# Splitting one weight load in two and moving its second half behind two others, at the start of a fused transformer block

## Chip, cores, metric

One core of one Trainium2 chip. The metric is the device time of one execution in microseconds (us), of the slowest (here the only) core. The profile's span, from the first to the last instruction, is about 1.8 us shorter than that time. Engines: PE multiplies matrices, PEld is its weight load, DVE, ACT and POOL are the vector, scalar and GpSimd engines; SP issues nearly all DMA. A load runs on 16 DMA engines; each signals when its part is in, and the load has landed with the sixteenth signal.

## The reference, cut to what matters

```python
mod = (_silu(c) @ w_mod).reshape(c.shape[0], 6, 1, -1)     # w_mod: 1024 x 6144
sa, ca, ga, sb, cb, gb = (mod[:, i].copy() for i in range(6))   # shortened
h = _layernorm(x) * (1 + ca) + sa
x = x + ga * linear_attention(h, wqkv, wo)      # x: 2048 x 1024, 32 heads
h = _layernorm(x) * (1 + cb) + sb
x = x + gb * swiglu(h, w_gate, w_up, w_down)    # inner width 3584
```

Everything is bf16. The change concerns `sa`, the shift of the first normalisation: a 1024 x 1024 block of `w_mod`, columns 0 to 1023, called wsa here.

## The kernel before: the parts concerned

A small scheduler records each operation and works out semaphore waits; all operations therefore carry one source line in the profile (L176), and one goes by the names of tiles. SP issues loads in program order:

```python
def sa_load(p):       # p = 0: columns 0-511, p = 1: columns 512-1023; 1 MB in rows of 1 KB
    P.dma("wsa%d" % p, WSA[:, :, 512 * p:512 * p + 512], wmv[:, :, 512 * p:512 * p + 512])
def wq_load(i, n=1):  # 256 KB per i, in rows of 2 KB
    P.dma("wq%d" % i, WQK[:, i:i + n, 0:D], wqkvv[:, i:i + n, 0:D])

ca_load(0); wq_load(0, 2); wq_load(2, 2); ca_load(1); wq_load(4, 2)
sa_load(1); wq_load(6); wq_load(7); sa_load(0)
for j in range(2):
    P.dma("x1_%d" % j, XRES[:, 4 + j, :], xv[:, 4 + j, :])
# ... more loads
```

PE uses wsa three times between parts of the first q product (`q_part`, one matmul of 512 columns for each column block nt and row block dt). `mod_sc` multiplies 128-column blocks of wsa by silu(c), with one moving column each; `bias_mm` folds the shift of row blocks 0 to 5 into a bias of q:

```python
for nt in range(7):
    if nt == 4:
        mod_sc(WSA, 0, range(6, 8))      # first use: columns 768-1023
        fin_sa(6, 2)                     # DVE copies the result out
        for dt in (6, 7): h0_scale(dt)   # DVE makes row blocks 6 and 7
    q_part(nt, qb[nt], (4, 5))
mod_sc(WSA, 0, range(4, 6))              # second use: columns 512-767
fin_sa(4, 2, True)
for nt in range(7):
    if nt == 2: bias_mm((4, 5))
    q_part(nt, qb[nt], (6,))
for nt in range(7):
    if nt == 1:
        mod_sc(WSA, 0, range(4))         # third use: columns 0-511
        fin_sa(0, 4, True)
        ln_ops[1][0](); ln_ops[1][1]()   # DVE statistics of the x load x1_1
    if nt == 4:
        bias_mm(range(4)); bias_fin()    # bias_fin: DVE copies the bias out
    q_part(nt, qb[nt], (7,))
# ... then the last column block of q, which needs the bank that the bias leaves
```

## Time and profile before

| | before |
|---|---|
| median of 3 runs | 830.8 us (830.74 to 831.32) |
| span, PE busy | 829.4 us, 823.2 us |
| right half of wsa: issue, landing | 7.79, 20.88 us |
| left half of wsa: issue to landing | 13.79, 11.5 us |
| PE at first, second, third use | 20.93, 22.64, 25.30 us |

The lines themselves stand in the prediction. They are read so: a `DMA` piece in the chain of waits ends where PE could go on; a row of the order of time gives the start of a group, its length, and in brackets the idle time ahead of it.

### The profile page before, as it was taken

How to read it: one execution, taken by the hardware profiler on the slowest of the kernel's cores; microseconds unless marked ns; L12 is line 12 of the kernel's file. 1: busy time of each engine (PE TensorE's matmuls, PEld its weight loads, DVE VectorE, ACT ScalarE, POOL GpSimd, SP SyncE). 2: the span in 40 equal slices, each digit the busy share in tenths (PEclk: the TensorE clock that was granted, in tenths of full speed). 3: DMA queues.
4: the chain of work that ended last, by engine and by line, in shares of the span. 5: the costliest groups of instructions: out<-in, count | busy, mean ns of one | idle time of the engine just before them, and what ended most of it. 6: DMA issues, size and time to landing. Idle time of an engine off the chain costs nothing.

```text
span 829.4 us, 10017 instructions
## 1 busy us (share of the span) xinstructions
PE 823.2 (99%) x4083; PEld 378.8 (46%) x4083; DVE 312.6 (38%) x665; ACT 197.5 (24%) x336; POOL 39.9 (5%) x57
## 2 busy tenths in 40 slices
PE   8999999999999999999999999999999999999998
PEld 4544444444444444444444444444444444444444
DVE  5797986756955521121221112122111211221111
ACT  4757641323242111011111101111110111111011
POOL 1010000000130000030000003000000300000000
PEclk9999999999999999999999999999999999999999
DMA  9969656938397985700455571045557004553000
GB/s 321 287 151 231 148 159 171 201 104 304 60 256 229 276 264 158 192 25 15 124 155 150 153 185 33 16 124 153 154 151 190 26 18 123 154 152 87 0 26 26
DMA packets 199246, 119.28 MB, mean 144 GB/s; under 512 B 57881, under 2 KB 182945, under 8 KB 199201
## 3 DMA queue, kind: packets, MB, share of 16 engines
q1 hardware_dynamic: 199184, 118.65, 52.8%
q8 instruction: 32, 0.52, 0.3%
q14 instruction: 14, 0.11, 0.0%
q10 hardware_dynamic: 16, 0.00, 0.0%
HBM read 100.67 MB, written 4.33 MB: 127 GB/s over the span
## 4 chain that ended last, share of the span: by engine, by line
PE 97%; DMA 2%; SPq 1%; issue 0%; DVE 0%
PE ps L176 97%; DMA wsa<-in_w_mod_dram 2%; SPq L176 1%; DVE xres L176 0%
## 5 line engine op out<-in xcount | busy, mean ns | idle before, releaser
L176 PE MATMUL ps<-h2t,gug 128*128 128x512 bf16 x896 | 211.7, 379 | 0.0
L176 PE MATMUL ps<-h2t,guu 128*128 128x512 bf16 x896 | 211.7, 379 | 0.0
L176 DVE TENSOR_TENSOR at<-sg,ps 128x512 bf16<-128x512 bf16 x112 | 77.0, 687 | 282.8 <-PE ps L176 281.2
L176 ACT ACTIVATE sg<-ps 128x512 bf16<-128x512 f32 x112 | 66.9, 597 | 309.7 <-PE ps L176 309.7
L176 PEld LDWEIGHTS ps<-h2t,guu 128*128 128x128 bf16 x896 | 87.6, 98 | 105.7
L176 PEld LDWEIGHTS ps<-h2t,gug 128*128 128x128 bf16 x896 | 87.7, 98 | 105.5
L176 PE MATMUL ps<-wd_a,at 128*128 128x512 bf16 (+1 forms) x512 | 112.4, 377 | 0.0
L176 PE MATMUL ps<-ht,wqk 128*128 128x512 bf16 x512 | 111.7, 379 | 0.0
L176 PE MATMUL ps<-wd_b,at 128*128 128x512 bf16 (+1 forms) x384 | 85.0, 377 | 0.0
L176 PEld LDWEIGHTS ps<-wd_a,at 128*128 128x128 bf16 x512 | 50.1, 98 | 59.6
L176 DVE TENSOR_TENSOR ut<-att,gb_b 128x512 bf16<-128x512 bf16 (+1 forms) x32 | 14.3, 447 | 166.8 <-ACT att L176 166.8
L176 PEld LDWEIGHTS ps<-ht,wqk 128*128 128x128 bf16 x512 | 49.5, 98 | 58.7 <-DVE biasq L176 0.2
L176 ACT ACTIVATE att<-ps 128x512 bf16<-128x512 f32 (+1 forms) x32 | 17.4, 591 | 182.1 <-PE ps L176 182.1
L176 PEld LDWEIGHTS ps<-wd_b,at 128*128 128x128 bf16 x384 | 37.6, 98 | 44.7
L176 PE MATMUL ps<-pk,xres 128*128 128x512 bf16 x256 | 56.5, 379 | 0.0
L176 PE MATMUL ps<-mw,pqt 128*128 128x512 bf16 x256 | 56.3, 379 | 0.0
L176 POOL TENSOR_SCALAR h2t<-h2t,modcol 128x512 bf16<-128x512 bf16 x32 | 26.3, 836 | 383.4 <-DMA h2t<-xn 383.4
L176 ACT ACTIVATE e<-ps 128x512 bf16<-128x512 f32 x56 | 33.1, 603 | 31.7 <-PE ps L176 19.8
L176 PEld LDWEIGHTS ps<-mw,pqt 128*128 128x128 bf16 x256 | 24.9, 98 | 30.2 <-DVE xres L176 0.4
L176 PEld LDWEIGHTS ps<-pk,xres 128*128 128x128 bf16 x256 | 24.9, 98 | 29.9 <-issue 0.4
L176 ACT ACTIVATE junk<-xres 128x1024 bf16<-128x1024 bf16 x24 | 25.4, 1058 | 35.1 <-DVE xres L176 34.9
L176 DVE SCALAR_TENSOR_TENSOR xres<-ps,xres 128x512 bf16<-128x512 f32 x32 | 21.4, 688 | 12.3 <-PE ps L176 11.5
(107 smaller groups left out, 344.8 us busy)
## 6 DMA issues: line engine op xcount, KB each, us to landing
gug<-in_B_w_gate_dram SPq DMA_DIRECT2D x56, 512.0 KB, 4.0
guu<-in_B_w_up_dram SPq DMA_DIRECT2D x56, 512.0 KB, 5.3
xres<-in_A_x_dram SPq DMA_DIRECT2D x20, 256.0 KB, 7.7
rb<-recip_den SPq DMA_DIRECT2D x8, 512.0 KB, 11.5
stgx<-in_w_mod_dram SPq DMA_DIRECT2D x2, 2048.0 KB, 7.9
wd_a<-in_B_w_down_dram SPq DMA_DIRECT2D x4, 1024.0 KB, 7.8
out_dram<-xres SPq DMA_DIRECT2D x31, 128.0 KB, 1.7
xres<-in_A_x_dram SPq DMA_DIRECT2D x3, 1024.0 KB, 14.1
```

What stands on the lines that cost most here:

```text
L176: return getattr(e, method)(**kw)
```

## The change

PE's first use needs only a quarter of wsa, columns 768 to 1023. The intent: load that quarter alone, so that the first use and q weights 6 and 7 get their data 0.5 MB sooner, and bring columns 512 to 767 behind them.

```diff
-        def sa_load(p):
-            P.dma("wsa%d" % p, WSA[:, :, 512 * p:512 * p + 512], wmv[:, :, 512 * p:512 * p + 512])
+        def sa_load(c0, c1):
+            P.dma("wsa%d" % c0, WSA[:, :, c0:c1], wmv[:, :, c0:c1])
 ...
-        sa_load(1)
+        sa_load(768, 1024)
         wq_load(6)
         wq_load(7)
-        sa_load(0)
+        sa_load(512, 768)
+        sa_load(0, 512)
```

## The prediction

> **What bounds the kernel now.** I read the page first, then the chain of waits that ended last, then the waits of the TensorE, then the order of time on PE and PEld between 17 and 28 us, then the times from DMA issue to landing, and last the DMA rate in stretches that carry rows of one length.
>
> ```profile
> PE 823.2 (99%) x4083; PEld 378.8 (46%) x4083; DVE 312.6 (38%) x665; ACT 197.5 (24%) x336; POOL 39.9 (5%) x57
> ```
>
> PE is busy 823.2 of 829.4 us. So only the few us of this span in which PE stands still can be won, and only from a wait that really stops it. The chain in order of time says where the last such wait is:
>
> ```profile
> 7.79 13.09 DMA wsa<-in_w_mod_dram
> 20.88 0.05 issue
> 20.93 805.88 PE ps L176 x3932
> ```
>
> The right half of the shift weights (wsa, columns 512 to 1023) is issued at 7.79 and lands at 20.88, PE starts at 20.93, and from there the chain is PE to the end. Whatever moves PE after 20.93 moves the end by as much, unless a later wait takes it back. The list of waits names that same load, for 0.2 us (`PE ps` waiting for `DMA wsa`), and no other load that the change touches. But the recorded length of a matmul is longer than its turn, so short stalls hide in it, and the starts have to be compared:
>
> ```profile
> 17.09 3.61 PE L176 MATMUL ps<-ht,wqk 128*128 128x512 bf16 x16
> 20.93 0.55 PE L176 MATMUL ps<-siluc,wsa 128*128 128x1 bf16 x16 [0.23 <-DMA wsa<-in_w_mod_dram]
> 21.34 1.46 PE L176 MATMUL ps<-ht,wqk 128*128 128x512 bf16 x6
> 22.64 0.54 PE L176 MATMUL ps<-siluc,wsa 128*128 128x1 bf16 x16
> 23.04 0.59 PE L176 MATMUL ps<-ht,wqk 128*128 128x512 bf16 x2
> 23.56 0.55 PE L176 MATMUL ps<-modtmp,wqk 128*128 128x1 bf16 x16
> 23.98 1.46 PE L176 MATMUL ps<-ht,wqk 128*128 128x512 bf16 x6
> 25.30 0.95 PE L176 MATMUL ps<-siluc,wsa 128*128 128x1 bf16 x32
> ```
>
> A matmul of 512 columns lasts 0.379 us in the record but starts 0.216 us after the one before: (3.61 - 0.379)/15 = 0.215. Sixteen of them from 17.09 put the next start at 17.09 + 16 x 0.2155 = 20.54. PE starts at 20.93: the real stall is 0.39 us, not 0.23. After the six from 21.34 the next start would be 22.64, and it is 22.64: the second use of wsa (columns 512 to 767) waits for nothing. After the six from 23.98 the next start would be 25.28, and it is 25.30. This third use, columns 0 to 511, looks free, but the weight loads say otherwise:
>
> ```profile
> 22.42 0.66 PEld L176 LDWEIGHTS ps<-siluc,wsa 128*128 128x128 bf16 x16
> 25.29 0.87 PEld L176 LDWEIGHTS ps<-siluc,wsa 128*128 128x128 bf16 x32 [0.35 <-DMA wsa<-in_w_mod_dram]
> ```
>
> At 22.42 the load of weights begins 0.22 ahead of its matmul, beside the matmul before it; at 25.29 it begins with its matmul, having waited for the DMA. Issue 13.79 plus 11.5 to landing is 25.29. So the left half of wsa lands just in time, with no slack at all.
>
> **What the Trainium skill says.** "TensorE: Matmul & The Clock Gate", section "Step-by-step: what each phase is for", gives about 216 ns between back-to-back matmuls of 512 columns and says that weight loads are pulled ahead of running matmuls; the trace agrees (0.2155 us, and 22.42 against 22.64). "Perfetto Trace Analysis", section "Optimization Strategies", says that splitting DMAs lets some start sooner where the DMA engines are generally idle. They are not idle here (windows below), so its condition fails. "DMA: Bandwidth & Descriptors", section "Specifications", puts line rate at 512 B and over; section "Why small descriptors are slow (HBM only)" counts about 3 cycles per packet on top of one per 32 B. By that, two of 512 B cost 2 x (16 + 3) = 38 cycles against 35 for one of 1 KB, 9% more (estimate). The trace disagrees on both:
>
> ```profile
> 25.40:26.80 1.40, 1.40 (x38) 1.04 (x37) 0.33 (x3) 0.85 (x1) 0.00 (x0) 1.00 1.10 352
> 236.00:241.00 5.00, 5.00 (x25) 2.29 (x24) 2.84 (x11) 1.78 (x3) 1.61 (x2) 1.00 1.20 290
> ```
>
> The last two columns are DMA share and GB/s. In the first stretch nearly all packets are rows of 1 KB (352 GB/s); in the second all are rows of 512 B, loads of gate and up weights with the very shape 128x8x256 that the change introduces (290 GB/s). Both keep the engines full, so shorter rows cost 21%.
>
> **The change part by part.** It removes one load of 1 MB in rows of 1 KB (512 bf16 columns) and adds two of 0.5 MB in rows of 512 B. The order of the instructions on PE, DVE, ACT and POOL stays; the first use now waits for columns 768 to 1023, and the second has a new wait, for columns 512 to 767.
> - Cost of a half: 524,288 B at 290 GB/s is 1.81 us, at 352 it is 1.49. The difference is 0.32; the issues of gate and up loads, 1.78 us apart in that full queue, give 0.29. I take 0.30 each, 0.60 for both.
> - First use: the loads ahead of it lose 0.5 MB, so it lands near 20.88 - 1.49 + 0.30 = 19.7, before 20.54. The stall of 0.39 is gone; PE reaches the second use at 22.64 - 0.39 = 22.25.
> - Second use: its load now stands at the byte position where q weights 7 end. These land at 22.26 before (issue 12.96, 9.3 to landing). With 0.60 for the short rows: 22.86, and a start at 22.91. New stall 0.66. The second use thus starts 0.27 later than before.
> - Third use: the work between second and third use took 25.28 - 22.64 = 2.64, so PE is there at 25.55. All bytes ahead of this load are the same as before, so it lands at 25.29 + 0.60 = 25.89. PE starts near 25.90 instead of 25.30. Further stall 0.35.
> - Sum: - 0.39 + 0.66 + 0.35, less the 0.02 that the old third use waited, is + 0.60 us. Behind it all loads are 0.6 later, but PE too, so no new wait arises there; 435 matmuls from 27.56 run at 0.2158 us each without a hole, so nothing absorbs the shift either. The extra issue, about 0.43 us on SP, lies in a queue that is full for 11 to 13 us ahead and is hidden.
>
> So the change takes a wait away from the first use and pays for it at the third, whose landing no order of the loads ahead can move: only their bytes and row lengths can. 830.8 + 0.6 = 831.4 us.
>
> **The rivals.** (1) Short rows cost nothing in this mix, as the line-rate figure would have it: then the second use stalls about 0.06, the third lands where it did, the 0.39 is given back there, and the time is 830.8. For it: two short loads stand between loads of 2 KB rows, not in a long run of short ones. Against it: 290 GB/s is steady over 6 us. (2) The gain of 0.39 is kept, 830.4. For it: the chain names only the first load. Against it: the left half's landing at 25.29 with the weight load waiting for it. (3) The short loads cost more than their bytes, since the engines finish unevenly or the two DMAs' completions lie in the path: up to twice my 0.6, 832.0. (4) A late shift makes another engine the bound (ACT and DVE are busy from 28 us with the activation of q): both move with PE, so I give it little.
>
> **Range and chances.** The three timed runs before lie between 830.74 and 831.32, and the mechanism can give between - 0.4 and + 1.2. Predicted 831.4, range 830.6 to 832.1. Two per cent is 16.6 us and the whole disputed stretch is some 5 us long: faster 0.005, same 0.985, slower 0.01.
>
> **What would show it.** In the new trace: no stall ahead of the first use, PE there at about 20.54; a wait of PE for wsa of about 0.66 ahead of the second use (start near 22.9) and one of about 0.35 ahead of the third (start near 25.9); windows with rows of 512 B at about 290 GB/s in the stretch from 15.5 to 21. It is wrong if the third use starts at 25.3 or before (rivals 1, 2), or if the shift of the third use isn't found again at the end.

## The result, and the profile after

The changed kernel took 832.09 us in the median of 6 runs (831.61 to 832.63), the kernel before 830.88 in 6 runs of the same rounds (830.53 to 832.01). The ratio is 1.0012 with a 95% interval of 1.0000 to 1.0025. (Ratios are from runs of the same rounds; they are not quite the quotient of the medians, nor of the plain means.) It is "the same" by the 2% rule, and inside the predicted range, though only 0.01 us under its upper end. Two more sets of the changed kernel, below, gave 1.0007 and 1.0004. The mean of the three is 1.0008, or 0.6 us, against the predicted 0.6; each interval alone reaches down to 1.0000 or below, so the times alone do not prove a cost; the profiles below have to.

First the page's line of busy times, the chain of waits in order of time, and the TensorE in order of time (start, length, group, idle time ahead), all of the changed kernel:

```profile
PE 824.1 (99%) x4083; PEld 378.7 (46%) x4083; DVE 312.0 (38%) x665; ACT 197.6 (24%) x336; POOL 40.1 (5%) x57
```

```profile
15.71 10.69 DMA wsa<-in_w_mod_dram
26.40 0.05 issue
26.44 801.70 PE ps L176 x3870
```

```profile
17.90 3.61 PE L176 MATMUL ps<-ht,wqk 128*128 128x512 bf16 x16
21.35 0.54 PE L176 MATMUL ps<-siluc,wsa 128*128 128x1 bf16 x16
21.75 1.46 PE L176 MATMUL ps<-ht,wqk 128*128 128x512 bf16 x6
23.56 0.55 PE L176 MATMUL ps<-siluc,wsa 128*128 128x1 bf16 x16 [0.36 <-DMA wsa<-in_w_mod_dram]
23.98 0.59 PE L176 MATMUL ps<-ht,wqk 128*128 128x512 bf16 x2
24.50 0.55 PE L176 MATMUL ps<-modtmp,wqk 128*128 128x1 bf16 x16
24.91 1.46 PE L176 MATMUL ps<-ht,wqk 128*128 128x512 bf16 x6
26.44 0.95 PE L176 MATMUL ps<-siluc,wsa 128*128 128x1 bf16 x32
```

The last DMA of the chain is now the left half of wsa, which lands at 26.40; before, it was the right half. From the starts: the first use comes at 17.90 + 16 x 0.2155 = 21.35, so without a stall. The second would come at 21.75 + 6 x 0.2155 = 23.04 and comes at 23.56: 0.52 us of stall. The third would come at 26.20 and comes at 26.44: 0.24. So far this is the predicted picture.

Two things in it were not predicted. PE is 0.81 us later already at 17.90 (17.09 before), ahead of any load that was changed. And the third use is 1.14 us later (26.44 against 25.30), not 0.6. The signals of the 16 DMA engines, which the trace records for each load, show why. This table is not a view of the page; it is worked out from those records (us; first, fifteenth and sixteenth signal):

```
                             before                  changed
load                     1st   15th   16th       1st   15th   16th
scale weights, 2nd half  14.15  14.82  14.96     14.05  15.63  16.75
q weights 4, 5           15.52  16.18  16.33     15.43  17.04  18.12
wsa 512-1023             18.43  19.11  20.88         -      -      -
wsa 768-1023                 -      -      -     17.21  19.82  20.33
q weights 6              19.11  19.79  21.56     17.89  20.51  21.01
q weights 7              19.79  20.48  22.24     18.59  21.21  21.74
wsa 512-767                  -      -      -     20.30  23.00  23.52
wsa 0-511                22.80  23.47  25.25     23.31  25.92  26.40
```

Read the first column of each for what the bytes and rows cost: the left half of wsa comes 23.31 - 22.80 = 0.51 us later on the engine that is first. Read the distance to the sixteenth for how far the slowest engine has fallen behind: 2.45 us before, 3.09 changed. PE waits for the sixteenth. In the kernel before, fifteen engines had delivered the right half by 19.11, well ahead of 20.54, where PE wanted it. A single engine, 1.77 us behind the others, made the stall that the change was meant to remove.

That engine lost its time in a step, between q weights 4 and 5 (0.15 us between fifteenth and sixteenth) and the right half of wsa (1.77). In that stretch the DMA view of the kernel before has one packet of another queue (queue and kind: packets, MB, share of 16 engines):

```profile
q1 hardware_dynamic: 508, 0.52, 104.6%
q8 instruction: 1, 0.02, 4.6%
```

It is one packet of 16 KB, from 16.05 us, and takes 1.10 us. The page counts 32 of them in the span. The Trainium skill, "Runtime: NRT & Kernel Launch", section "Instruction fetch mechanics", says that each engine's instructions are refilled in blocks of 16 KiB (256 instructions) by a DMA queue of its sequencer, and that crossing a block is "mostly hidden". PE has 2 x 4083 = 8166 weight loads and matmuls, which would be 32 blocks (an estimate from the page's figure); that these packets are PE's instructions is inferred from this count, not shown. In the changed kernel such a packet came at 16.80 us and met another engine than the slowest: the fifteenth signal moves away from the first between q weights 4 and 5 and wsa 768-1023 (from 1.61 to 2.61 us). The slowest engine there was already behind, after the first x loads, where one packet of 2 KB took 1.00 us.

So a third term stands beside bytes and rows: the lag of the slowest of 16 engines, which differs from run to run.

### The profile page after: what moved, and what is told of

Same layout as the page of the kernel before. It is cut to its first block, busy times and chain, and to the rows that moved or that the text cites. A ratio compares the mean times of both kernels' runs of the same rounds, so it can differ in the third digit from the quotient of the medians.

```text
span 830.7 us, 10019 instructions
## 1 busy us (share of the span) xinstructions
PE 824.1 (99%) x4083; PEld 378.7 (46%) x4083; DVE 312.0 (38%) x665; ACT 197.6 (24%) x336; POOL 40.1 (5%) x57
## 4 chain that ended last, share of the span: by engine, by line
PE 97%; SPq 2%; DMA 1%; issue 0%; DVE 0%
PE ps L176 97%; SPq L176 2%; DMA wsa<-in_w_mod_dram 1%; DVE xres L176 0%
```

## The experiments

Theories, as the expectations call them. **A**: the end is set by the landing of the left half of wsa at the third use; short rows make it 0.5 to 0.6 us later, and the slowest engine's lag comes on top. **L**: short rows also make the slow engine fall further behind. **O**: not the rows but the new order, with its wait at the second use, is what costs. **N**: there is only noise, or something else sets the end. Theories **B** (half clock) and **F** (the instruction packet makes the lag) came up on the way. Times are medians, and each set was timed against the kernel before on the same chip.

**1 and 2. Both kernels again.** No edit.

> The kernel before, unchanged, as a second look. Theory A: the end is set by the landing of the left half of the shift weights at the third use on PE, and that landing is the time of the slowest of 16 DMA engines: one engine falls about 1.8 us behind the other 15 when the 16 KB packet on the instruction queue (near 16 us) takes its turn on it. Expected: ratio 1.000 (within 0.0006); in the trace again one engine that signals 1 to 3 us after the other fifteen for the load of the right half, on whichever engine the instruction packet hits; the first of the 16 signals of the third load near 22.8, the last between 24.5 and 26.5, and PE's third use within 0.1 us behind that last one. Rival N (noise alone): no such lone engine.

> The changed kernel again. Theory A: first signal of the third load near 23.3 (0.5 later than before, the price of 2048 short rows), the lag of the slowest engine 1.5 to 3.2 us as in any run, time +0.5 to +0.7 us over the kernel before (ratio 1.0006 to 1.0008). Rival L (short rows also make the slow engine fall further behind, by some 0.3 to 0.6 us more): +0.9 to +1.3 us (1.0011 to 1.0015). Rival N: ratio 1.000.

Before again: 831.1 us, ratio 1.0001 (0.9989 to 1.0013). Left half: first signal 22.89, last 25.11; third use 25.16. Here the lag is spread over several engines (the fifteenth signals at 24.11), so "one lone engine" was too simple, but the sixteenth again decides. Changed again: 831.38 us, ratio 1.0007 (0.9995 to 1.0019). First signal 23.53, last 25.27: later rows, but a lag of only 1.74 us, and the third use at 25.41 without any stall (24.12 + 6 x 0.2155 = 25.41). Its five runs fall into two heaps, 831.25 to 831.38 and 832.34 to 832.36. That fits A, but with an interval from 0.9995 it does not exclude N. It speaks against L: the lag was smaller than before's, not larger. Over all 14 profiles of this document the lag at the left half is 2.38 us in the mean of the 7 with short rows and 2.25 in that of the 7 without, which is much less than its scatter.

**3. Short rows alone, old order.**

```diff
         sa_load(768, 1024)
+        sa_load(512, 768)
         wq_load(6)
         wq_load(7)
-        sa_load(512, 768)
```

> Short rows alone: both halves of the right half in loads of their own, but both ahead of q weights 6 and 7 as before. Theory A: the third load lands as in the changed kernel, so the same time as the changed kernel, +0.5 to +0.7 us, though the stall now stands at the first use (near 0.9 us) and there is none at the second. Rival O (the new order, with its wait at the second use, is what costs): ratio 1.000. Rival L: as the changed kernel, +0.9 to +1.3.

832.02 us, ratio 1.0024 (1.0002 to 1.0046), with a first signal of the left half at 23.44 and the third use at 25.78, 0.5 us later than before. The cost of the rows is there without the new order, so O falls. There was no stall at the first use (20.89), against the expectation: this time the last signal of both quarters was in by 21.04, and PE needs only the first, in at 19.48. The mean is drawn up by two of six runs, of 833.71 and 838.31 us, with a mean clock of 0.998 and 0.996 where the others of the set have 1.0; the other four have a mean of 831.67, 0.54 above that of the kernel before (831.13). Even so, 838.31 is not explained by its clock alone, and no profile of it was kept.

**4. All four quarters short.**

```diff
-        sa_load(0, 512)
+        sa_load(256, 512)
+        sa_load(0, 256)
```

> The changed kernel with the left half (columns 0 to 511) split into two loads of 512 B rows too: 4096 short rows in place of 2048. Theory A: first signal of the last quarter near 23.8, time +1.1 to +1.3 us over before (twice the price of short rows, 1.0013 to 1.0016). Rival O or N: no more than the changed kernel. Rival L: +1.8 or more.

833.54 us, ratio 1.0022 (1.0009 to 1.0035), more than A allowed. First signal of the last quarter 24.26 (expected 23.8), 1.46 us later than before, so about 0.36 for each short load. The third use came at 26.06, only 0.76 us later than before's, because the lag happened to be 1.76. But from there to the end this profile took about 2 us more than the others. Engines' busy times by stretch (the last three columns are granted clock, DMA share, GB/s) say why:

```profile
25.00:28.60 3.60, 2.86 (x70) 2.06 (x70) 1.43 (x4) 1.87 (x3) 0.00 (x0) 1.00 1.09 357
28.70:32.00 3.30, 3.30 (x10) 1.22 (x8) 2.70 (x12) 3.30 (x8) 1.14 (x2) 0.50 1.07 365
```

After the stall at the third use PE's clock was granted at half, for 3.413 us. At half speed that costs 1.7 us. Three of the five runs had it (mean clock 0.998: 833.54 to 834.11), two did not (831.48, 832.70). This is theory B, made after the fact; runs 5 and 6 test it. (Another 0.38 us of this profile is a wait near 147 us, see run 9.)

**5 and 6. The third use later, without short rows.** The kernel before, with the left half behind one or two x loads of 256 KB.

```diff
-        sa_load(0)
         for j in range(2):
             P.dma("x1_%d" % j, XRES[:, 4 + j, :], xv[:, 4 + j, :])
+            if j == 0: sa_load(0)        # third_late_1
+        sa_load(0)                       # third_late_2: here instead
```

> The kernel before (rows of 1 KB), with the left half of the shift weights behind one x load of 256 KB (rows of 2 KB). Only the landing of the third use moves, by 0.68 us (the distance of the landings of q weights 6 and 7 in the trace of before). Theory A (that landing sets the end): PE's third use near 25.9 and +0.6 to +0.8 us, ratio 1.0007 to 1.0010. Theory B, on top of A (a stall of PE of about 0.9 us there drops its clock to half for 3.4 us, as in the profile of the kernel with all rows short): in some runs another 1.7 us with a mean clock of 0.998. Rival N (something else than the third use sets the end): 1.000.

> The same, behind two x loads of 256 KB: the landing moves by 1.36 us. Theory A alone: third use near 26.6, +1.3 to +1.5 us, ratio 1.0016 to 1.0018, clock 1.0. Theory B: the stall of about 1.3 us drops the clock in all or nearly all runs: +3.0 to +3.3 us, ratio 1.0036 to 1.0040, mean clock 0.998, with a stretch of 3.4 us at 0.5 from about 28 to 32 us. Rival N: 1.000.

One load: 832.05 us, ratio 1.0011 (0.9998 to 1.0024); three runs at full clock of 831.57 to 832.05, two at 0.998 of 833.18 and 833.55. Two loads: 834.28 us, ratio 1.0029 (1.0016 to 1.0043); four runs at 0.998 of 833.79 to 835.20, one at full clock of 832.45. The rows for two loads, TensorE in order of time and the stretch behind it:

```profile
24.25 1.45 PE L176 MATMUL ps<-ht,wqk 128*128 128x512 bf16 x6
26.72 0.95 PE L176 MATMUL ps<-siluc,wsa 128*128 128x1 bf16 x32 [1.02 <-DMA wsa<-in_w_mod_dram]
```

```profile
29.30:32.60 3.30, 3.30 (x10) 1.10 (x9) 2.48 (x12) 3.18 (x6) 1.07 (x2) 0.50 1.09 357
```

The third use moved to 25.96 and 26.72, each right behind the sixteenth signal (25.91 and 26.68). The full-clock runs (three and one) have medians of 831.64 and 832.45, only 0.25 and 1.06 us above the median before (831.39), less than A's 0.6 and 1.3.

The profiles settle it better: from the start of the third use to the last instruction it is 804.05 to 804.25 us in two profiles of the kernel before, two of the changed one (the first two) and that of run 7, and 805.79 and 805.81 here, 1.7 more, as 3.413 us at half clock cost. So in these profiles A and B both hold: the end moves with the third use, and the half clock comes on top. The stall there was 0.66 us with one x load (25.96 against 24.01 + 6 x 0.2155 = 25.30), a kernel with the half clock in 2 of 5 runs, and 1.18 us with two, in 4 of 5. But a late third use is not the only way to it. A mean clock of 0.998, as 3.413 us at half give it over the span, also stands in one of 51 timed runs of the kernel before (833.42 us) and in single runs of 3, 8, 10 and 12.

The Trainium skill, "TensorE: Matmul & The Clock Gate", section "Why this matters for your kernels", asks for no idle gaps above about 3 us. The 3.413 us agree with the window of 3413 ns in the page's section "What's actually happening"; that it takes 3 us of idle does not agree with these runs. Nor does the length of the stall decide: a profile of the changed kernel (below) had 0.92 us of it at the second use and kept its clock.

What trips it was not tested, but the traces give a lead. In the three traces with the half clock, the record of full clock ahead of it lasts 20.48, 20.48 and 23.89 us, which is 6, 6 and 7 times 3.413, from a start that differs from run to run: a grid of steps of 3.413 us that does not begin with the kernel. In the stretch of this grid just ahead of the half clock PE started 5 (run 4; one of them is missing in the record), 6 and 5 (runs 5 and 6) matmuls of 512 columns; in the eight other traces with clock records no stretch from 16 us on had fewer than 7. (Ahead of 16 us, among transposes, stretches with 5 or 6 kept the clock.) So the same stall may or may not trip it, by where it falls on the grid, which would explain why only some runs of a kernel are hit.

**7. The instruction packet earlier.** The kernel before, with more and shorter warming matmuls:

```diff
-        warm(13, bank=3)
+        for _ in range(52):     # 128 columns instead of 512
+            P.pe("matmul", out=PS[:, 3, 0:128], lhsT=IDENT[:], rhs=E1[:, 0, 0:128], start=True, stop=True)
```

> The kernel before with the 13 warming matmuls of 512 columns replaced by 52 of 128 columns: the same work in time, 39 more pairs of weight load and matmul, so the 16 KB packet on the instruction queue should come 39 pairs earlier in the program, near 11 to 12 us instead of 16. Theory F (that packet is what sets one of the 16 DMA engines back): the engine falls behind in the second load of scale weights (last signal 1 to 1.8 us later than in before, near 16.3 to 16.8) and no new lag arises in the load of the right half; a further such packet near 23 to 25 us. Time within 1 us of before. Rival (the lag belongs to the load of shift weights or to chance): the second load of scale weights lands near 15.0 to 15.4 as before, and the step stands between 16 and 20 us again.

831.37 us, ratio 0.9998 (0.9985 to 1.0012). The packet came earlier, at 14.23 us, though not at 11 to 12. The DMA view from 14 to 15.5 us, where before had no such line:

```profile
q1 hardware_dynamic: 353, 0.54, 101.7%
q8 instruction: 1, 0.02, 4.7%
```

With it the slowest engine's step moved: from first to sixteenth signal, the lag was 1.45 us at the second half of the scale weights, 2.15 at q weights 4 and 5, 2.22 at the right half of wsa. Before, it was 0.81, 0.81 and 2.45. So the step now stands where q weights 4 and 5 land, one load earlier, and there is none behind it; it is smaller, 0.70 us. That supports F; it is one profile, and the predicted place was wrong by 2 to 3 us.

**8. A version meant to beat both: q weights 7 behind the left half,** rows of 1 KB, first use one matmul later, third use one earlier.

```diff
-        wq_load(7)
         sa_load(0)
+        wq_load(7)
 ...
-                if nt == 4:
+                if nt == 5:
                     mod_sc(WSA, 0, range(6, 8))
 ...
-                if nt == 1:
+                if nt == 0:
                     mod_sc(WSA, 0, range(4))
 ...                                          # and bias_mm(range(4)) at nt == 3
```

> A version meant to beat both, with rows of 1 KB: the left half of the shift weights ahead of q weights 7, so that it lands 0.68 us earlier (near 24.5); on PE the first use one matmul later and the third use one matmul earlier, ahead of the first product with q weights 7. Theory A: no stall at the third use, 0.1 to 0.2 left at the first; -0.2 to -0.4 us against before, ratio 0.9995 to 0.9998. If a lagging engine makes q weights 7 late: 0 to -0.2. Rival N: 1.000.

831.45 us, ratio 1.0004 (0.9992 to 1.0017), one run of five at 0.998. In the profile no use of wsa waits, but the second half of the scale weights landed at 16.44 (lag 2.37 us) and PE was 0.5 us late from there on. No gain.

**9. The changed kernel a third time.**

> The changed kernel a third time, for the size of its cost, which the two earlier sets put at 0.12% and 0.07%. Theory A: ratio 1.0006 to 1.0012, clock 1.0 in nearly all runs (its stalls at second and third use are under 0.7 us each), first signal of the left half's load 23.3 to 23.6, last 25.2 to 26.6, PE's third use right behind the last. Rival N: 1.000.

831.98 us, ratio 1.0004 (0.9992 to 1.0016), under the 1.0006 that A expected. First signal of the left half 23.26, last 25.93, third use 25.98. Second use at 23.06 where it would have come at 20.85 + 6 x 0.2155 = 22.14: 0.92 us of stall, against the expectation of under 0.7. And this profile has a wait that the other two of the changed kernel do not have, in the time order of PE:

```profile
147.58 20.89 PE L176 MATMUL ps<-pk,xres 128*128 128x512 bf16 x96 [0.56 <-DVE g L176]
```

PE loses 0.73 us here, waiting for DVE (tile g), DVE for ACT, and ACT for a load of other data (zb). That load was issued 1.68 us and landed 1.90 us later than in the kernel before, while PE was only 0.84 us later by then. The wait stands in three of the seven profiles with short rows (0.73, and 0.38 and 0.55 in runs 4 and 10) and in none of the seven without; whether the short rows bring it or chance is not shown.

**10. The same order as in 8, with short rows** (the diff of 8 applied to the changed kernel).

> The changed kernel with its short rows, but q weights 7 behind the left half of the shift weights and the third use one matmul earlier on PE, the first one later. The left half lands 0.68 us earlier than in the changed kernel. Theory A: the cost of the short rows at the third use is gone or nearly so: ratio 1.0000 to 1.0005, as in the same order with rows of 1 KB, and at least 0.3 us under the changed kernel of this set. Rival (the short rows cost elsewhere): ratio as the changed kernel, 1.0007 to 1.0012.

832.19 us, ratio 1.0011 (0.9994 to 1.0027), so not under the changed kernel (831.98); one of six runs, of 835.72, was at 0.998. The profile shows a wait that I had overlooked, first on DVE, then on PEld:

```profile
27.39 1.29 DVE L176 BATCH_NORM_STATS2 stats<-xres 128x6 f32<-128x512 bf16 x2 [0.79 <-DMA xres<-in_A_x_dram]
28.59 0.15 DVE L176 COPY biasq<-ps 128x8 f32<-128x8 f32 x1
```

```profile
28.79 0.76 PEld L176 LDWEIGHTS ps<-ht,wqk 128*128 128x128 bf16 x5 [0.69 <-DVE biasq L176]
```

DVE works in program order. Its statistics of the next x load stand ahead of the copy of the q bias, that x load lands late, and PE waits for the copy.

**11 and 12. That wait taken away,** by placing the two statistics behind the copy, in 8 and in 10.

```diff
                     fin_sa(0, 4, True)
-                    ln_ops[1][0]()
-                    ln_ops[1][1]()
 ...
                     bias_fin()
+                    ln_ops[1][0]()
+                    ln_ops[1][1]()
```

> As the version with q weights 7 behind the left half (rows of 1 KB), and on DVE the two statistics instructions that wait for the next x load now come behind the copy of the q bias instead of ahead of it: in the short-row version of that order the copy stood 0.79 us behind an x load that landed late, and PE waited for it. Theory A: the last product before the activation of q no longer depends on an x load; -0.2 to -0.4 us against before, ratio 0.9995 to 0.9998, and no run with the half clock. Rival N: 1.000.

> The same with the short rows of the changed kernel. Theory A: the short rows' 0.6 us is covered by the 0.68 us that the left half lands earlier: ratio 0.9997 to 1.0003, within 0.3 us of the same version with rows of 1 KB, and PE does not wait for the copy of the q bias. Rival (the short rows cost elsewhere): +0.6 us or more over the version with rows of 1 KB.

Both missed: 831.95 us, ratio 1.0009 (0.9995 to 1.0023), and 832.97 us, ratio 1.0020 (1.0007 to 1.0032; one of five runs at 0.998). PE no longer waits for wsa or for the bias, but what it won is given back. The rows of PEld at 45 us, with rows of 1 KB (version 11) and then in the kernel before:

```profile
44.85 0.10 PEld L176 LDWEIGHTS ps<-ht,wqk 128*128 128x128 bf16 x1 [0.23 <-DVE ht L176]
45.17 0.10 PEld L176 LDWEIGHTS ps<-ht,wqk 128*128 128x128 bf16 x1 [0.23 <-DVE ht L176]
45.50 0.10 PEld L176 LDWEIGHTS ps<-ht,wqk 128*128 128x128 bf16 x1 [0.23 <-DVE ht L176]
```

```profile
44.61 2.47 PEld L176 LDWEIGHTS ps<-ht,wqk 128*128 128x128 bf16 x12
```

Here PE takes the next 512 rows of x, one row block after the other as DVE scales them, at 0.32 us each instead of 0.2155. DVE itself had waited for the transposes of those rows, which depend on the same stream of x loads. In version 11 this and one gap at 31 us take back some 0.6 us. So behind the wait for wsa stands a second bound, about half a microsecond away, fed by the same loads. The time of version 12 is not fully explained: its profiled run was of 832.3 us, and its slower runs have no profile. No version beat the kernel before.

## Why the prediction was right, point by point

- **The bound, and that the third use decides: right.** In the profiles of both kernels and of runs 3 to 6, the third use starts within 0.15 us of the sixteenth signal of its last load, or right at PE's own pace. Moving that landing moved the end (runs 5 and 6), and behind it the time to the end is the same within 0.2 us in five profiles without another wait.
- **The cost of the rows: right, 0.30 each predicted.** On the first engine, the short load ahead of q weights 6 takes 1.78, 1.81 and 1.73 us between signals in three profiles, the one behind q weights 7 1.71, 1.67 and 1.74. Half of the long load takes (18.43 - 15.52)/2 = 1.46. The excess is 0.32 and 0.25 in the mean. The first signal of the left half is 0.51, 0.64 and 0.46 us later than in the profiles of before (22.80 and 22.89, in the order of the sets, the third against the first).
  The windows in the changed kernel:

```profile
15.50:17.00 1.50, 1.50 (x9) 0.69 (x7) 0.00 (x0) 0.00 (x0) 0.00 (x0) 1.00 1.22 326
19.00:20.50 1.50, 1.50 (x9) 0.68 (x8) 0.00 (x0) 0.00 (x0) 0.00 (x0) 1.00 1.14 298
```

  They do not test the predicted 290 GB/s: by bytes only 66% and 58% of them are short rows, the rest rows of 2 KB and 1 KB. The signals do: 0.5 MB of short rows in 1.67 to 1.81 us is 290 to 314 GB/s.
- **First use free: right.** No stall in three profiles.
- **Second use 0.66, third use 0.35 of stall: right in kind, wrong in size.** Second: 0.52, 0, 0.92, in the mean 0.48. Third: 0.24, 0, 0.28, in the mean 0.17. They follow the lag and the time at which PE arrives.
- **PE at 20.54 at the first use: wrong by -0.09 to 0.81.** It was 21.35, 21.09 and 20.45. The step that failed is "All bytes ahead of this load are the same as before, so it lands at 25.29 + 0.60", and with it "only their bytes and row lengths can" move the landing. The runs showed a term beside these: the lag from first to sixteenth signal, 2.45 and 2.22 us before, 3.09, 1.74 and 2.67 changed. It alone makes the third use scatter from 25.41 to 26.44, more than the change does.
- **Nothing behind takes or gives: nearly right in two profiles, wrong in the third.** The claim was that "no new wait arises there". In the first and the third profile 0.1 to 0.2 us were lost near 45 us, in short gaps of the kind shown for version 11; in the third another 0.73 us at 147 us (run 9). So of the 1.5 us by which that profile is longer than the kernel before, only 0.68 lie at the third use.
- **Sum.** + 0.6 us predicted; + 0.6 is the mean of three sets (1.0012, 1.0007, 1.0004). The first set's 832.09 is 0.7 above the predicted 831.4. That the sum fits so closely is in part luck: the price of the rows (0.57 against 0.60) is measured, but the gain of 0.39 at the first use did not come as predicted. PE reached it at 20.96 in the mean, as late as before with its stall, and the stalls behind it were smaller by about as much (0.65 together against 1.01). The rival that the rows cost nothing is refuted by the signals; the one that the 0.39 us gain is kept is, too. The half clock was no rival of mine, and could have made the prediction wrong: it did not occur in the 16 runs of the changed kernel, but in one of 51 of the kernel before and in runs 3 to 6, 8, 10 and 12.

## What to carry to other kernels

A wait for a load is a wait for the slowest of its DMA engines: before reordering loads for a few tenths of a microsecond, look at the first and the last signal, since a lag of one engine is not cured by moving bytes of all. Splitting a load in a full queue by columns shortens its rows, and every load behind it pays; look for the last use in line, because a gain at the first is given back there. And keep a margin where PE's work is thin: a stall of about a microsecond can, in some runs, cost another 1.7 in clock.

## What the Trainium skill lacked or had wrong

- "DMA: Bandwidth & Descriptors", section "Specifications", has line rate from 512 B up. Measured: rows of 512 B at 290 to 314 GB/s (window and signals), of 1 KB at 352, with the engines full in both. The per-packet count of "Why small descriptors are slow (HBM only)" gives 9% (estimate in the prediction), the runs 17 to 22% (0.25 to 0.32 us on 1.46).
- "Runtime: NRT & Kernel Launch", section "Instruction fetch mechanics", calls the refill of instructions mostly hidden. Measured beside a full queue: one packet of 16 KB takes 1.10 us on one DMA engine, which then delivers 1.62 us further behind the other fifteen (from 0.15 to 1.77), and every later load waits for it. That the packet is the cause rests on its time, on its moving with the step in run 7, and not on a run without it.
- "TensorE: Matmul & The Clock Gate", section "Why this matters for your kernels", sets the limit of harmless gaps near 3 us. Measured: stalls of 0.66 to 1.18 us amid matmuls of one column were followed by 3.413 us at half clock in three profiles, of kernels with a lower mean clock in 2 to 4 of 5 runs.
- No page that I read has how far the 16 engines' signals for one load lie apart in a full queue: 0.8 us at best, 1.7 to 3.1 at the left half of wsa, changing from run to run.
